# A longer token gather in the model that orders an attention and mixture-of-experts kernel

## The chip, the cores and the metric

The kernel runs on one core of one Trainium2 chip. A core has five engines that run side by side, each through its own list of instructions in a fixed order: TensorE (PE in the profile; its weight loads are PEld), VectorE (DVE), ScalarE (ACT), GpSimd (POOL) and SyncE (SP). They wait for each other by semaphores. Transfers are started by SP (hardware queue, q1) and by POOL (software queue, q0). The metric is device time in microseconds, median of several runs.

## The reference

Eight batches of eight heads of attention over 576 positions, half the heads with a window of 32, half with a dilated window of 128 with every fourth position; the result is a table of 4608 tokens of 512 numbers. A router then gives each token to one of eight experts of at most 576 tokens each, greedily by the largest logit, and each expert is a two-layer network:

```python
logits = x @ w_gate
order = np.argsort(-logits.flatten())
for idx in order:
    tok, e = (int(idx) // E, int(idx) % E)
    if assigned[tok] >= 0 or counts[e] >= cap:
        continue
    assigned[tok] = e
    counts[e] += 1
...
for e in range(E):
    mask = assigned == e
    out[mask] = np.maximum(x[mask] @ w1[e], 0.0) @ w2[e]
```

## The kernel before, in words

The first 230 us are attention. It leaves the tokens in a table `xd` in HBM and the logits on the chip. Then come eight rounds, one per expert.

In a round r the router **searches** which expert fills up next and down to which logit it accepts. The search is a chain that goes to and fro: TensorE counts (`pz<-G,ohr`, L782, nine small matmuls), VectorE narrows the interval (from `Q`, L819, to a new `G`, L796) and TensorE counts again, eight times. At its end VectorE makes the flags `ge` (L991) and the rank of each chosen token is counted on TensorE (L1028, L1029). VectorE turns ranks into places: `scan` (L1036) to `oa` (L1074), and six writes `ob` (L1087). GpSimd and ScalarE each scale half of `oa` into `rx` (L1079, L1083). Eighteen small matmuls `ptx<-rx,ob` (L1094) then put the token numbers in order; this is the **listing**. VectorE makes the index list `idx` of it (L1106).

GpSimd **gathers** the 576 tokens of the list from `xd` by five indirect transfers (`xg<-xd,idx`, L1258: four of 128 rows and one of 64). TensorE **turns** each of the five by four transposes into the one bank `ptx` (L1272); ScalarE copies it out as `xh` and VectorE writes the remainder `xl` (both by L1141 and L1142). A turn waits until the turn before it was copied out.

The **first product** is L1309: for each of eight slices f of the hidden layer, tokens 0 to 255 into `ph0` and 256 to 575 into `ph1`, twelve matmuls each (weights split in `w1h` and `w1l`, tokens in `xh` and `xl`). ScalarE and VectorE make `hb` of it (L1141, L1329). The **second product** is L1351: for each of five token blocks m and each f three matmuls into `py0` or `py1` in turn (L1354 and L1356 for the last block of 64). ScalarE copies `py` to `y` and GpSimd scatters it to the output (L1377).

The weights come from HBM into `raw` (SP, L1159). ScalarE makes the high half `w1h` or `w2h`; the low half is written by VectorE, or, in three cases among them both layers of the second expert, by a ScalarE copy (L1167) and an adding transfer of GpSimd (`w1l<-raw`, L1169). In the second round the loads of slices 4 to 7 of `w1` wait for a small memset on GpSimd (L1150, the gate) behind the second gather.

No order of instructions is written by hand. Every step is an `op` with an engine, an assumed cost, an assumed latency `lat` (after the engine is free again, until others see the result), the ops it depends on, and a boost. `Schedule.run` first goes through the ops backwards and gives each the time `left` to the end along its longest path; `due` is the end less `left` less the boost. Then it plays the engines forward in its own time: on each engine it takes the ready op with the earliest `due`, or another that fits in front of it. Whatever comes out of that is the order in which the instructions stand on the engines. `T_G` is the latency of the gathers in this model; it is in no instruction. The model takes 1250 ns of GpSimd for a gather, and then `lat`.

Of the kernel before, what the change touches and what calls it, by code (L numbers as in the profile page):

```python
# [37 lines left out]
T_P, T_S, AHEAD = 440, 2150, 5  # L38
B_L, B_G, B_T, B_X, B_H, B_HL, B_Y, B_S, B_W = 23000, 27000, 15000, 0, 20000, 17000, 28000, -15000, 1500
RAW1, D_R, NQ, AHEAD_W = 8, 262, (2, 2), (3, 4)  # L40
ADDED, T_A, T_G = (("2", 0), ("1", 1), ("2", 1)), 4500, 4500
NS, B_E, DIRECT = (2, 2), 3000, 7
B_C = (0, 2500, 20000, 20000, 20000, 20000, 20000, 20000)
P_U, B_A, B_K, B_V, B_P, TOL_A, TOL_B, TOL_C, TOL_D = 4680, 15400, -5200, 14500, -105500, 650, 650, 300, 800
# [111 lines left out]
class Schedule:  # L156
# [8 lines left out]
    def op(self, eng, cost, fn, deps=(), boost=0, lat=0, dma=0, buf=None):  # L165
        x = Op(len(self.ops), eng, cost, fn, deps, boost, lat, dma, buf)
        for d in x.deps:
            d.users.append(x)
        self.ops.append(x)
        return x  # L170
# [940 lines left out]
def moe(tc, ctx, C, R, xd, w1, w2, out):  # L1111
# [8 lines left out]
    op = K.op  # L1120
# [130 lines left out]
    def gather(r, ix, box):  # L1251

        done = []
        for m, n in enumerate(MSZ):
            xg, old, use = XG.take()

            def get(xg=xg, n=n, m=m):
                nc.gpsimd.indirect_dma_start(out=xg[:n], out_offset=None, in_=xd,  # L1258
                                             in_offset=bass.IndirectOffsetOnAxis(ap=box[0][:n, m:m + 1], axis=0))

            g = op("POOL", 1250, get, [ix, *old], B_G, lat=T_G if r else 2500)
            got[r, m] = g
            if r == 0:
                pt, old, usep = (PYR if m % 3 < 2 else PTR).take()
            else:
                pt, old, usep = PTR.take()
            pt = pt.rearrange("p (d x) -> p d x", d=ND)
            a, b = (x[:, :, 128 * m:128 * m + n] for x in (XH, XL))

            def turn(pt=pt, xg=xg, n=n):  # L1270
                for d in range(ND):
                    nc.tensor.transpose(pt[:, d, :n], xg[:n, 128 * d:128 * d + 128], C["identf"][:n, :n])  # L1272

            t = op("PE", 460 if n == 128 else 250, turn, [g, *old], B_T)
            use.append(t)
            if r == 0:
                turns.append(t)
            full = 500 if n == 128 else 290
            wx = x_users.get((r - 1, 0 if m < 2 else 1), [])
            s0 = op("ACT", full, lambda pt=pt, a=a, n=n: act(a, pt[:, :, :n]), [t, *wx], B_T)  # L1280
            s1 = op("DVE", full + 100, lambda pt=pt, a=a, b=b, n=n: sub(nc.vector, b, pt[:, :, :n], a), [s0], B_T)
            usep += [s0, s1]
            done.append((s0, s1))
        return done
# [107 lines left out]
    def round_(r):  # L1392
        e = None
        if r:
            e = search(r) if r < NE - 1 else chain("DVE", 650, R.last, [st["fetch"], st["need"]])
        en = st["fetch"] = EN[r] = op("SP", 100, lambda: fetch(r, R.eidx), [e])
        ix, BOX[r] = settle(r, e)
        X[r] = gather(r, ix, BOX[r])
        W[r] = [weights("1", r, f, [en]) for f in range(NF)]
# [85 lines left out]
```

## Time and profile before

| what | value |
|---|---|
| runs before | 704.34 us median of 3 (703.73 to 706.86) |
| the profiled execution | 708.44 us, of which the span of its instructions is 706.6 us |
| TensorE matmuls, weight loads | 665.0 us (94 %), 585.0 us (83 %) |
| VectorE, ScalarE, GpSimd | 484.7 us (69 %), 291.4 us (41 %), 140.6 us (20 %) |
| mean granted TensorE clock | 0.972 of full speed |

The profile comes from one execution. Times in it count from the start of its span. A row of the timeline has the start, the duration, the engine, the line, the operation and what it writes from what; in brackets stands how long the engine sat idle before it and what ended that. Matmuls overlap: their durations are longer than the distance from one start to the next, and it is the distance that adds up. The first round's tokens are turned from 236 us on, the first expert's products lie between 240 and 304 us, the second's between 304 and 357 us.

### The profile page before, as it was taken

To read this page: it belongs to the slowest core of one execution; us is meant where nothing else is said; L and a number is where in the kernel's file an instruction comes from. 1 tells how busy PE (TensorE), PEld (TensorE's weight loads), DVE (VectorE), ACT (ScalarE), POOL (GpSimd) and SP (SyncE) were. 2 spreads that over 40 slices of the span, in tenths; PEclk is the share of its full clock that TensorE was granted. 3 is DMA by queue.
4 is the path that set the end of the run, shared out by engine and by line. 5 is a ranking of instruction groups with operands and counts; after the bars stand their busy time and mean duration, and the time that the engine had idled before them with its cause. 6 is when DMAs were issued, how large, how long until landed. Compare 5 with 4: busy or idle time off the path is not lost.

```text
span 706.6 us, 17388 instructions
## 1 busy us (share of the span) xinstructions
PE 665.0 (94%) x6579; PEld 585.0 (83%) x6581; DVE 484.7 (69%) x2086; ACT 291.4 (41%) x616; POOL 140.6 (20%) x206
## 2 busy tenths in 40 slices
PE   7899999999974899899999999999999999999995
PEld 5787899888963698699889889879978988988983
DVE  5467877789457889588689879969978854724200
ACT  3344554453521474286335434423524525424210
POOL 6111111100000332452410410310321131211011
PEclk9999999999985899999999999999999999999998
DMA  9999999973211684889314514512711574113001
GB/s 253 266 265 284 279 311 255 264 202 80 63 41 45 194 177 112 249 174 268 98 53 137 180 51 130 185 43 73 239 51 53 164 261 147 50 58 98 1 23 45
DMA packets 58524, 104.60 MB, mean 148 GB/s; under 512 B 6212, under 2 KB 27844, under 8 KB 58436
## 3 DMA queue, kind: packets, MB, share of 16 engines
q1 hardware_dynamic: 49096, 78.32, 38.7%
q0 software_dynamic: 9344, 25.17, 13.4%
q8 instruction: 51, 0.84, 0.5%
q14 instruction: 33, 0.27, 0.1%
HBM read 78.31 MB, written 18.87 MB: 138 GB/s over the span
## 4 chain that ended last, share of the span: by engine, by line
PE 68%; issue 12%; DVE 10%; POOL 3%; DMA 3%; ACT 1%; another core or an unknown queue 1%; POOLq 0%; SPq 0%; DVEq 0%
PE py L1351 18%; PE ph L1309 17%; PE pS L506 9%; PE px L514 6%; PE px L564 3%; PE pS L503 3%; PE pm L486 2%; PE ptx L1272 2%; PE pz L782 2%; PE py L1354 1%; PE py L1356 1%; POOL out L1377 1%; DVE hb L1329 1%; DVE G L796 1%; DMA qs<-in_qd 1%
## 5 line engine op out<-in xcount | busy, mean ns | idle before, releaser
L1351 PE MATMUL py<-w2h,hb 128*128 128x512 f32 x512 | 172.0, 401 | 0.0
L1309 PE MATMUL ph<-xh,w1h 128*128 128x256 f32 (+1 forms) x512 | 138.1, 300 | 0.0
L1309 PE MATMUL ph<-xl,w1h 128*128 128x256 f32 (+1 forms) x512 | 136.8, 298 | 0.0
L1309 PE MATMUL ph<-xh,w1l 128*128 128x256 f32 (+1 forms) x512 | 136.0, 296 | 0.0
L1351 PEld LDWEIGHTS py<-w2h,hb 128*128 128x128 f32 x512 | 96.7, 189 | 19.4
L1351 PE MATMUL py<-w2l,hb 128*128 128x512 f32 x256 | 100.2, 392 | 0.0
L1141 ACT ACTIVATE hb<-ph 128x256 fp32r<-128x256 f32 (+2 forms) x192 | 59.6, 345 | 88.5 <-PE ph L1309 86.9
L1309 PEld LDWEIGHTS ph<-xh,w1h 128*128 128x128 f32 x512 | 91.8, 190 | 0.5
L1309 PEld LDWEIGHTS ph<-xh,w1l 128*128 128x128 f32 x512 | 91.8, 190 | 0.1
L1309 PEld LDWEIGHTS ph<-xl,w1h 128*128 128x128 f32 x512 | 91.4, 190 | 0.1
L506 PE MATMUL pS<-q,k 128*80 128x96 f32 (+1 forms) x672 | 83.0, 265 | 0.0
L1377 POOL DMA_INDIRECT out<-y,idx x40 | 41.3, 1034 | 194.6 <-ACT y L1141 136.0
L456 ACT ACTIVATE E<-pS 96x384 f32<-96x384 f32 (+1 forms) x96 | 46.5, 486 | 75.2 <-PE pS L506 74.1
L1329 DVE SCALAR_TENSOR_TENSOR hb<-ph,hb 128x320 fp32r<-128x320 f32 (+1 forms) x128 | 57.0, 452 | 29.4 <-ACT hb L1141 25.2
L506 PEld LDWEIGHTS pS<-q,k 128*80 128x80 f32 (+1 forms) x672 | 68.5, 158 | 0.0
L1141 ACT ACTIVATE y<-py 128x512 f32<-128x512 f32 (+1 forms) x40 | 23.8, 596 | 104.0 <-PE py L1351 90.5
L493 DVE CUSTOM_DVE_ANT_0 junkm<-pm,const 128x80 bf16<-128x80 f32 (+1 forms) x336 | 59.5, 244 | 4.2 <-PE pm L486 3.6
L1351 PEld LDWEIGHTS py<-w2l,hb 128*128 128x128 f32 x256 | 48.6, 190 | 8.5
L514 PE MATMUL px<-v,E 81*64 81x65 f32 (+1 forms) x1344 | 47.9, 225 | 5.3 <-issue 2.9
L1258 POOL DMA_INDIRECT xg<-xd,idx x40 | 42.1, 1054 | 52.7 <-PE ph L1309 25.1
L514 PEld LDWEIGHTS px<-v,E 81*64 81x64 f32 (+1 forms) x1344 | 42.8, 138 | 10.2 <-issue 3.8
L1141 ACT ACTIVATE w1h<-raw 128x512 fp32r<-128x512 f32 x64 | 39.6, 628 | 27.6 <-DMA raw<-in_moe_w 27.2
(179 smaller groups left out, 1009.5 us busy)
## 6 DMA issues: line engine op xcount, KB each, us to landing
raw<-in_moe_w SPq DMA_DIRECT2D x128, 256.0 KB, 4.6
v<-in_vp SPq DMA_DIRECT2D x8, 780.0 KB, 14.2
v<-in_vd SPq DMA_DIRECT2D x8, 650.0 KB, 10.3
xd<-xs SPq DMA_DIRECT2D x16, 288.0 KB, 7.5
xd<-xs SPq DMA_DIRECT2D x32, 144.0 KB, 9.2
w2l<-raw POOLq DMA_DIRECT2D x16, 256.0 KB
qs<-in_qp SPq DMA_DIRECT2D x7, 576.0 KB, 10.1
k<-in_kp SPq DMA_DIRECT2D x7, 576.0 KB, 9.7
```

What stands on the lines that cost most here:

```text
L456: e = self.op("ACT", 380, lambda j=j, pS=pS: nc.scalar.activation(self.E[:self.nk, j * self.gs:j * self.gs + self.gs], pS.tile[:, :self.gs ...
L493: nc.vector.tensor_tensor_reduce(out=jk[:, c - c0, :nk], in0=pm[:, (c - c0) * nk:(c - c0 + 1) * nk], in1=mm[:, min(1, (c if self.kind == 0 ...
L503: nc.tensor.matmul(pS[:nk, c - c0], ls[:64 + n, c], self.r[:64 + n, :2 * nq], start=(c == c0), stop=False, skip_group_check=True)
L506: nc.tensor.matmul(pS[:nk, c - c0], self.Ks[c], self.Qm[c], start=False, stop=True, skip_group_check=True)
L514: nc.tensor.matmul(px[64 * a:64 * a + 64, c - c0], lh, self.V[c][a], start=True, stop=True)
L564: nc.tensor.transpose(t[:, c], src, C["identf"])
L1141: act = lambda o, i, f=AF.Copy: nc.scalar.activation(o, i, f)
L1258: nc.gpsimd.indirect_dma_start(out=xg[:n], out_offset=None, in_=xd, in_offset=bass.IndirectOffsetOnAxis(ap=box[0][:n, m:m + 1], axis=0))
L1309: nc.tensor.matmul(o, a[:, d * 128:d * 128 + 128], b[:, d, c0:c1], start=((d, i) == pairs[0]), stop=((d, i) == pairs[-1]))
L1329: hl = op("DVE", 335 if j == 0 else 400, lambda: nc.vector.scalar_tensor_tensor(hb[:, CAP + c0:CAP + c1], o, 0.0, hb[:, c0:c1], op0=OP.max ...
L1351: nc.tensor.matmul(py, x, w, start=(f + i == 0), stop=(f == NF - 1 and i == 2))
L1377: s = nc.gpsimd.indirect_dma_start(out=out, out_offset=bass.IndirectOffsetOnAxis(ap=box[0][:n, m:m + 1], axis=0), in_=y[:n], in_offset=None)
```

## The change

The tuple `T_G` now holds three latencies: 2500 ns for the first round, as before, 7000 ns for the second, where it was 4500 ns, and 4500 ns for all later rounds, as before.

```diff
-ADDED, T_A, T_G = (("2", 0), ("1", 1), ("2", 1)), 4500, 4500
+ADDED, T_A, T_G = (("2", 0), ("1", 1), ("2", 1)), 4500, (2500, 7000, 4500)
...
-            g = op("POOL", 1250, get, [ix, *old], B_G, lat=T_G if r else 2500)
+            g = op("POOL", 1250, get, [ix, *old], B_G, lat=T_G[min(r, 2)])
```

The instructions are the same, 5688 rows on TensorE before and after. The order differs on TensorE, VectorE, ScalarE and GpSimd, on TensorE from the first expert's first product (some 249 us in the profile) to the second expert's second product (some 345 us); after that, and on SP throughout, it is the same. In the first product the last six of the eight counts L782 of the second round's search stand 12 to 18 matmuls earlier; the last of them stood behind the first three matmuls of the second product, and stands now behind the third matmul of the last group of the first product (`ph1`, f = 7).

On TensorE, the first expert's second product, before. `w2h6` and `hb6` are the weights and the hidden layer of slice f = 6, `py0` and `py1` the banks of the token blocks, `ge` the flags, `rx` and `ob` the listing's inputs; each pair of a weight and a hidden slice stands for three matmuls.

```order
L1351 MATMUL py0_3208<-w2h6_3237,hb6_3268 128x512
...
L1351 MATMUL py0_3208<-w2h7_3238,hb7_3269 128x512
...
L1028 MATMUL pz_81<-ge_4244,const4_64 128x72
...
L1351 MATMUL py1_3209<-w2h0_3231,hb0_3262 128x512
...
L1351 MATMUL py0_3208<-w2h0_3231,hb0_3262 128x512
...
L1094 MATMUL ptx0_3210<-rx_4289,ob_4293 128x40
```

And now:

```order
L1351 MATMUL py0_3208<-w2h4_3235,hb4_3266 128x512
...
L1028 MATMUL pz_81<-ge_4237,const4_64 128x72
...
L1351 MATMUL py0_3208<-w2h5_3236,hb5_3267 128x512
...
L1351 MATMUL py0_3208<-w2h6_3237,hb6_3268 128x512
...
L1094 MATMUL ptx0_3210<-rx_4273,ob_4277 128x40
...
L1351 MATMUL py0_3208<-w2h7_3238,hb7_3269 128x512
...
L1351 MATMUL py1_3209<-w2h0_3231,hb0_3262 128x512
```

The ranks L1028 moved up by three slices (nine matmuls), the listing L1094 by 30 matmuls. Between the two there were 27 matmuls, and there are six. The slice f = 7 of the first token block stands behind the listing. On VectorE the last write of `hb` for that slice (L1329, 128x320) stands now behind the six `ob`; it stood ahead of the search's last step.

On GpSimd, from the last adding transfer of the first expert to the gate of the second round (`raw_3215` is the buffer of slice 4); + and - are the difference from before to now, `y_3271` to `y_3273` are finished token blocks on their way out:

```order
 L1169 DMA w1l_3239<-raw_3211 128x512
 L1169 DMA w1l_3240<-raw_3212 128x512
 L1169 DMA w1l_3241<-raw_3213 128x512
-L1376 MEMSET spacer 1x1
-L1377 DMA out<-y_3272,idx 4608x512
 L1258 DMA xg_3255<-xd,idx 128x512
 L1258 DMA xg_3256<-xd,idx 128x512
...
+L1169 DMA w1l_3242<-raw_3214 128x512
+L1377 DMA out<-y_3271,idx 4608x512
+L1377 DMA out<-y_3272,idx 4608x512
 L1150 MEMSET raw_3215 1x1
```

The scatters of the first two token blocks stood ahead of the gathers, the first of them ahead of the three adding transfers as well; now both, and a fourth adding transfer, stand between the gathers and the gate.

On ScalarE, the copies `xh` of the turns among the second expert's weights, before (`raw14` to `raw16` are the slices f = 4 to 6, whose loads wait for the gate):

```order
L1141 ACTIVATE xh_3260<-ptx0_3210 128x4x128 x2
L1141 ACTIVATE w1h4_3227<-raw14_3215 128x512
L1141 ACTIVATE y0_3271<-py1_3209 128x512
L1167 ACTIVATE w1l4_3243<-w1h4_3227 128x512
L1141 ACTIVATE w1h5_3228<-raw15_3216 128x512
L1141 ACTIVATE xh_3260<-ptx0_3210 128x4x128
```

And now:

```order
L1141 ACTIVATE xh_3260<-ptx0_3210 128x4x128 x2
L1141 ACTIVATE y2_3273<-py0_3208 128x512
L1141 ACTIVATE w1h4_3227<-raw14_3215 128x512
L1141 ACTIVATE xh_3260<-ptx0_3210 128x4x128
L1167 ACTIVATE w1l4_3243<-w1h4_3227 128x512
L1141 ACTIVATE w1h5_3228<-raw15_3216 128x512
L1167 ACTIVATE w1l5_3244<-w1h5_3228 128x512
L1141 ACTIVATE w1h6_3229<-raw16_3217 128x512
L1141 ACTIVATE xh_3260<-ptx0_3210 128x4x128
```

The third copy `xh` stood behind the conversions of slices 4 and 5, and stands behind that of slice 4; the fourth stands behind that of slice 6, ahead of which it stood. The five turns themselves stand earlier in the second product on TensorE: the first is behind slice 3 of the third token block (it was behind slice 2 of the fourth), the fourth behind slice 3 of the fourth block.

## Rows read from the trace of the kernel before

**Rows 1.** The page: the span, and busy time by engine.

```profile
span 706.6 us, 17388 instructions
PE 665.0 (94%) x6579; PEld 585.0 (83%) x6581; DVE 484.7 (69%) x2086; ACT 291.4 (41%) x616; POOL 140.6 (20%) x206
```

**Rows 2.** The waits of TensorE: who waited for what, us in total, times, the longest. The first two are all that there is from 240 to 305 us, the third all from 305 to 345 us, the last all from 345 us to the end.

```profile
PE pz L782 <- DVE G L796: 2.7, 1, 2.7
PE ptx L1272 <- DVE xl L1142: 0.5, 1, 0.5
...
PE pz L1028 <- DVE ge L991: 0.6, 1, 0.6
...
PE ptx L1094 <- DVE ob L1087: 0.5, 2, 0.2
```

**Rows 3.** The chain that ended last, in order of time, around 290 us: start, us, what.

```profile
288.02 0.82 DVE G L796
...
288.98 3.63 another core or an unknown queue
```

**Rows 4.** Busy time by stretch: from and to, length, then busy us (and instructions) of PE, PEld, DVE, ACT and POOL, the granted TensorE clock, the DMA share, GB/s.

```profile
291.90:294.80 2.90, 0.24 (x2) 0.11 (x2) 1.98 (x9) 0.60 (x1) 0.35 (x1) 1.00 1.01 242
295.70:298.60 2.90, 2.89 (x9) 2.51 (x10) 2.45 (x10) 1.12 (x2) 0.00 (x0) 0.52 1.03 395
```

**Rows 5.** Timeline of TensorE.

```profile
262.46 0.45 PE L782 MATMUL pz<-G,ohr 128*128 128x64 bf16 x9
...
266.01 0.46 PE L782 MATMUL pz<-G,ohr 128*128 128x64 bf16 x9
...
268.86 0.39 PE L1351 MATMUL py<-w2h,hb 128*128 128x512 f32 x1
...
269.56 0.47 PE L782 MATMUL pz<-G,ohr 128*128 128x68 bf16 x9
...
274.05 0.39 PE L1351 MATMUL py<-w2h,hb 128*128 128x512 f32 x1
...
275.00 0.19 PE L1028 MATMUL pz<-ge,const 128*128 128x72 bf16 x1
...
275.06 0.47 PE L1351 MATMUL py<-w2h,hb 128*128 128x512 f32 x1
...
281.31 0.62 PE L1094 MATMUL ptx<-rx,ob 128*128 128x40 bf16 x18
281.78 0.48 PE L1351 MATMUL py<-w2h,hb 128*128 128x512 f32 x1
...
289.11 0.46 PE L782 MATMUL pz<-G,ohr 128*128 128x64 bf16 x9
289.41 0.63 PE L1272 MATMUL ptx<-const,xg 128*128 128x128 f32 x4
289.79 0.47 PE L1351 MATMUL py<-w2h,hb 128*128 128x512 f32 x1
...
291.72 0.40 PE L1351 MATMUL py<-w2h,hb 128*128 128x512 f32 x1
294.78 0.46 PE L782 MATMUL pz<-G,ohr 128*128 128x64 bf16 x9 [2.66 <-DVE G L796]
295.71 1.11 PE L1272 MATMUL ptx<-const,xg 128*128 128x128 f32 x4 [0.47 <-DVE xl L1142]
```

**Rows 6.** Timeline of VectorE.

```profile
269.64 0.49 DVE L1329 SCALAR_TENSOR_TENSOR hb<-ph,hb 128x320 fp32r<-128x320 f32 x1 [0.26 <-ACT hb L1141]
...
274.71 0.23 DVE L991 TENSOR_TENSOR ge<-te,gg 128x72 bf16<-128x72 f32 x1
...
277.45 3.50 DVE L1087 TENSOR_TENSOR ob<-si,const 128x384 bf16<-128x384 int32 x6
...
283.16 0.33 DVE L1106 SCALAR_TENSOR_TENSOR idx<-t 64x5 int32<-64x5 f32 x2
...
292.63 0.32 DVE L819 STREAM_TRANSPOSE Q<-pz 128x128 f32<-128x128 f32 x1 [3.65 <-remote]
...
294.97 0.68 DVE L1142 TENSOR_TENSOR xl<-ptx,xh 128x512 fp32r<-128x512 f32 x1
```

**Rows 7.** Timeline of ScalarE.

```profile
292.69 0.60 ACT L1141 ACTIVATE xh<-ptx 128x512 fp32r<-128x512 f32 x1 [4.83 <-remote]
...
297.35 0.63 ACT L1141 ACTIVATE w1h<-raw 128x512 fp32r<-128x512 f32 x1
```

**Rows 8.** Timeline of GpSimd.

```profile
283.84 1.03 POOL L1258 DMA_INDIRECT xg<-xd,idx  x1 [0.30 <-DVE A L1053]
...
289.86 0.09 POOL L1150 MEMSET raw<- 1x1 f32 x1
...
291.22 1.03 POOL L1377 DMA_INDIRECT out<-y,idx  x1 [0.27 <-issue]
```

**Rows 9.** SP's loads of weights: first the timeline (start, us until the next is issued), then the DMA view of 289 to 296 us (count, size of one, median us from issue to landing).

```profile
289.97 0.33 SPq L1159 DMA_DIRECT2D raw<-in_moe_w  x1
...
raw<-in_moe_w SPq DMA_DIRECT2D x8, 256.0 KB, 5.9
```

## The prediction

> **What bounds the kernel now.** I read the busy times first, then the waits of TensorE, then the timeline of the one stretch that the change reorders. TensorE is busy for 665.0 of 706.6 us [rows 1], and the list of its waits is short: 4.3 us in all from 240 us to the end, of which 0.5 us lie after 345 us [rows 2]. So the mixture-of-experts part is a queue of matmuls with next to no gaps, in which the search, the listing and the gathers of the next expert run beside the products of this one. From that two things follow. A better order has at most those few microseconds to win. And since the order after the second expert is the same as before and holds no slack (0.5 us of waits), what is lost in the changed stretch is not made up later.
>
> The largest wait is odd. At 288.98 us the chain names no engine for 3.63 us [rows 3]; VectorE (`Q`) sat idle for 3.65 us and ScalarE (`xh`) for 4.83 us, and both went on within 0.06 us of each other [rows 6, 7], though the count and the turn that they follow had begun at 289.11 and 289.41 us and last 0.46 and 0.63 us [rows 5]. TensorE ran out of work for it: 2.66 us without a matmul, until 294.78 us [rows 5]. From 295.70 to 298.60 us its granted clock was 0.52, against 1.00 around it: the lower of the two levels, 1.2 instead of 2.4 GHz. That cost 2.9 x 0.48 = 1.4 us more [rows 4]. Together 4.1 us.
>
> The profiled execution took 708.44 us: 706.6 us of span and 1.84 us around it. The median of the runs is 704.34 us, 4.1 us less. I therefore take it that the odd wait is an event of the profiled execution and not of the usual run, and count it out: 708.44 - 4.1 = 704.3 us is the base. That is a choice; the other reading is a rival below.
>
> **The change part by part.** The new latency costs nothing by itself, no instruction is added or gone. All that counts is where TensorE now meets a result that isn't there yet.
>
> *Units.* Between 275.06 and 281.31 us lie 27 matmuls of the second product, so one takes 0.2315 us; between the counts at 262.46 and 266.01 us lie 24 of the first product and one count of 0.30 us, so one takes 0.135 us; a turn takes 0.38 us, the listing 0.47 us (281.31 to 281.78) [rows 5].
>
> *The search, earlier.* The last count stood at 269.56 us, three matmuls into the second product. It now stands nine matmuls of 320 columns (by columns 0.15 us each, 1.3 us) and those three (0.7 us) earlier: 267.55 us, and the second product begins at 268.86 + 0.30 = 269.16 us. From the last count to the ranks L1028 the chain over VectorE took 275.00 - 269.56 = 5.44 us, so the ranks can be counted at 273.0 us. TensorE is at their new place after 15 matmuls, at 269.16 + 3.47 = 272.6 us, and waits 0.4 us. Whether VectorE can keep up with counts that come up to 2.4 us sooner is the unknown here: by its busy share it has little room, and if the search didn't get earlier at all, the ranks would come at 275.0 us as before and everything below 2.0 us later. I take the full 2.0 us, since VectorE waits for the count in this stretch more often than the count for VectorE.
>
> *The listing, too early.* From the ranks to the end of the six `ob` (277.45 + 3.50 = 280.95 us) VectorE needs 5.95 us [rows 5, 6], and the listing needs all six. Before, 27 matmuls (6.25 us) stood between, which covered it: the listing began at 281.31 us without a wait. Now six stand there, 1.39 us. TensorE has done them at 273.0 + 0.06 + 1.39 = 274.45 us, and the last `ob` is there at 273.0 + 5.95 = 278.95 us: a stop of 4.5 us, in which only the listing's own first matmuls run. Behind it stands slice 7 of the first token block, and it must wait for the last `hb`, which VectorE now writes after the `ob`, 0.49 us [rows 6]: it starts at 279.5 us. Before, it started at 274.05 us, with 0.80 us of work and wait still to come that now lies behind it (ranks 0.33 us with their wait, listing 0.47 us). TensorE is 279.5 - 274.05 - 0.8 = **4.65 us** late. Bounds: 4.0 us if VectorE is a little quicker, 6.7 us if the search gains nothing.
>
> *The clock.* The stop is longer than the one before 294.78 us, which was followed by 2.9 us at the lower level [rows 4, 5]. So the clock should fall here too. Part of the low stretch may lie in the stop itself, where it costs nothing, so the price is between 0 and 1.4 us; I take **1.0 us**, nearer to the row. The Trainium skill says the same against the change (TensorE: Matmul & The Clock Gate, section "Why this matters for your kernels": no gaps between bursts of matmuls, or the array falls back to the half clock); the trace agrees, with 0.52 after the one long gap. By that rule alone, with the low stretch wholly behind the stop, the sum would be 0.4 us higher.
>
> *The gathers and the gate.* The list `idx` came 1.7 us after the listing's end, with VectorE still at other work before it; the first gather was issued at 283.84 us, 2.06 us after that end [rows 5, 6, 8]. Now the listing ends at 279.05 us, so the first gather goes out near 280.9 us, three microseconds earlier. The turns need no gather for long: the first turn found its tokens 5.57 us after the issue (283.84 to 289.41) without a wait, and it will come at 290 us or later. So what 7000 ns stands for in the model costs TensorE nothing here, before or after.
>
> The gate is another matter. It stood right behind the gathers, 6.02 us after the first [rows 8]. Now an adding transfer and two scatters with their small memsets stand in front of it. From the gate to the end of the next scatter, 291.22 + 1.03 = 292.25 us, one adding transfer and one scatter took 2.39 us; with a second scatter of 1.3 us that is 3.7 us. The gate comes at 280.9 + 6.0 + 3.7 = 290.6 us, a little later than before (289.86 us), though the gathers are earlier. The load of slice 4 starts 0.1 us behind it and takes 5.9 us [rows 9]: 296.6 us. On ScalarE the third `xh` now stands behind the conversion of that slice, and the fourth turn needs it: 0.63 + 0.60 us on ScalarE [rows 7], 0.68 us for `xl` [rows 6], 0.2 us to hand over: 298.7 us. TensorE gets to the fourth turn after 63 matmuls (14.6 us), three counts and three turns (2.0 us) and the 1.0 us of clock: 279.5 + 17.6 = 297.1 us. It waits 1.6 us, less the 0.5 us for `xl` which the old order paid [rows 2]: **1.1 us**. Bounds: a gain of 0.5 us if the load is quick, 4 us if the load takes the 7.4 us from its issue to the conversion in the trace (289.97 to 297.35 us, where ScalarE was held up by the odd wait).
>
> *The second expert's first product.* Three counts of the third round's search stand closer together than before (the sixth to the seventh 20 matmuls apart instead of 28), and the ranks cost 0.6 us of wait before [rows 2]. I take **0.3 us**, bounds -0.6 and 1.5 us.
>
> Sum: 708.44 - 4.1 + 4.65 + 1.0 + 1.1 + 0.3 = 711.4 us, 7.0 us or 1.0 % over the median before.
>
> **The rivals.** A difference of 0.5 % is 3.5 us here, about what can be told from none: "same" is 700.8 to 707.9 us.
>
> *The odd wait belongs to every run before* (it stands between the search and the first turn, in a stretch of dense transfers), and the new order, which has other work there, doesn't meet it. Then the median of 704.34 us holds it, and the result is 704.34 - 4.1 + 7.05 = 707.3 us. For it: it hits two engines at one point of the order. Against: the 4.1 us between the profile and the median, and the lowest run, 703.73 us, is near it. Chance 0.17, half of it within "same", since its own error is some 1.5 us.
>
> *It is met again after, or the fourth turn waits for the long load*: 711.4 + 3 to 4 = 715 us. Chance 0.12.
>
> *The stop is a loan* (faster). The listing is late because its chain is; if the search were done by 268.5 us, the `ob` would be there at 274.45 us, TensorE would not stop, and the earlier gathers would clear the waits of 0.5 and 4.1 us: 704.3 - 0.5 = 703.8 us, or 699.7 us with the odd wait in the median. The mechanism is the whole search moving by 4.5 us more; it decides from a last count at 263.1 us. Against it: the place of that count in TensorE's list, which fixes it at 267.5 us or later. Chance 0.05.
>
> *The order changes and nothing shows*, because the work in the stretch is the same and other waits shrink by as much: 704.3 us. Waits of TensorE that could shrink are 4.3 us in all, most of it the odd one. Chance 0.06.
>
> **How the numbers follow.** The forecast, with its own range of 708.5 to 714 us, has 0.60. Of the last two rivals together (0.11) some 0.05 falls below 700.8 us: faster 0.05. Same: half of the first rival (0.085) and the other 0.065 of the last two: 0.15. Slower: the rest, 0.80. The range for 8 in 10 leaves out the last two rivals and the upper half of the second: 705.5 to 714.5 us.
>
> **What would show it.** In the profile after: TensorE idle for 4 to 5 us before L1094 near 274 to 279 us, named `ob` or `rx` as what ended it; a granted clock near one half for some of the 3 us after; a first gather near 281 us and a gate (L1150) near 290.6 us, behind two scatters; a wait of the fourth turn for `xl`, with ScalarE's conversion of slice 4 in front of `xh`; the second expert's first product beginning some 6 us later than in a run before without the odd wait, and no wait after 345 us that differs from before. I'm wrong if the listing starts without a stop, or if the later experts make the time good, or if the odd wait turns out to be in the usual run.

## The result, and the profile after

The changed kernel takes 711.0 us (median of 19 runs, 705.7 to 717.4) against 704.2 us of the kernel before on the same chip: the ratio is 1.0088, with a 95% interval of 1.0068 to 1.0109, so 4.8 to 7.7 us slower. The forecast was 711.4 us. Two more series of the same kernel on another chip gave 1.0102 (1.0063 to 1.0141) and 1.0088 (1.0057 to 1.0119).

The profiled execution of the changed kernel took only 705.72 us, with a span of 703.9 us; that of before took 708.44 us. The difference lies ahead of the change: the first round's ranks (L1028) stood at 220.51 us here and at 224.90 us in the profile of before, and over all profiles of this study they lie between 219.7 and 229.0 us whatever the kernel. So everything below is counted from these ranks. To set a time of this profile beside one of [rows 5 to 9], add 4.39 us to it.

The waits of TensorE in the kernel after, from 240 to 305 us (who waited for what, us in total, times, the longest):

```profile
PE ptx L1094 <- POOL rx L1079: 2.0, 1, 2.0
PE ptx L1094 <- DVE ob L1087: 1.1, 5, 0.2
PE pz L1028 <- DVE ge L991: 0.2, 1, 0.2
```

The wait of 2.7 us for `G` and that of 0.5 us for `xl` [rows 2] are gone; the listing waits in their place. TensorE's timeline there:

```profile
268.94 0.19 PE L1028 MATMUL pz<-ge,const 128*128 128x72 bf16 x1 [0.16 <-DVE ge L991]
...
270.23 0.39 PE L1351 MATMUL py<-w2h,hb 128*128 128x512 f32 x1
272.65 0.23 PE L1094 MATMUL ptx<-rx,ob 128*128 128x40 bf16 x3 [2.04 <-POOL rx L1079]
273.07 0.24 PE L1094 MATMUL ptx<-rx,ob 128*128 128x40 bf16 x3 [0.19 <-DVE ob L1087]
...
274.94 0.24 PE L1094 MATMUL ptx<-rx,ob 128*128 128x40 bf16 x3 [0.23 <-DVE ob L1087]
275.03 0.53 PE L1351 MATMUL py<-w2h,hb 128*128 128x512 f32 x1
```

The six matmuls behind the ranks are through at 270.46 us (270.23 us and the 0.23 us that one takes); the listing's 18 matmuls come in six small pieces, each as its `ob` is written, and the product goes on at 275.03 us. The stop lasts 4.57 us. The first and longest wait in it, 2.04 us, ends with `rx` of GpSimd, which starts as soon as VectorE has written `oa`; the five after it end with one `ob` each. The last `ob` is there at 274.89 us and so sets the end of the stop; `hb` and the list follow. VectorE and GpSimd (timelines):

```profile
271.39 3.50 DVE L1087 TENSOR_TENSOR ob<-si,const 128x384 bf16<-128x384 int32 x6
274.81 0.48 DVE L1329 SCALAR_TENSOR_TENSOR hb<-ph,hb 128x320 fp32r<-128x320 f32 x1
...
275.74 0.33 DVE L1106 SCALAR_TENSOR_TENSOR idx<-t 64x5 int32<-64x5 f32 x2
```

```profile
271.56 1.03 POOL L1079 TENSOR_TENSOR rx<-oa,const 128x360 bf16<-128x360 bf16 x1 [12.21 <-DVE oa L1074]
```

Behind the stop the clock is down. Busy time by stretch, columns as in [rows 4]; the granted clock is the third figure from the right:

```profile
270.46:275.00 4.54, 1.41 (x18) 0.84 (x18) 4.47 (x11) 4.38 (x8) 2.76 (x4) 1.00 0.65 170
275.00:277.50 2.50, 2.50 (x10) 1.96 (x11) 2.25 (x9) 1.42 (x3) 1.90 (x2) 0.56 1.00 166
277.50:280.00 2.50, 2.50 (x10) 2.00 (x9) 1.84 (x7) 1.16 (x1) 1.97 (x2) 0.75 0.87 200
280.00:283.00 3.00, 3.00 (x15) 2.48 (x14) 0.00 (x0) 0.00 (x1) 2.39 (x4) 1.00 0.66 193
```

That costs 2.5 x 0.44 + 2.5 x 0.25 = 1.7 us. Then the gathers, the gate and the loads; timeline of GpSimd, of SP, and the DMA view of 284 to 294 us, to be read beside [rows 8, 9]:

```profile
276.34 1.08 POOL L1258 DMA_INDIRECT xg<-xd,idx  x1 [0.52 <-DVE cap L1019]
...
285.43 0.97 POOL L1377 DMA_INDIRECT out<-y,idx  x1 [0.22 <-issue]
286.40 0.09 POOL L1150 MEMSET raw<- 1x1 f32 x1
```

```profile
raw<-in_moe_w SPq DMA_DIRECT2D x8, 256.0 KB, 4.6
```

The gate stands 10.06 us behind the first gather, after two scatters; the loads behind it took 4.6 us in the median, not 5.9, the first of them (slice 4, which the fourth turn needs) 3.2 us, and no turn waits. From the first ranks to the end of the span this execution took 483.4 us, that of before 481.7 us, although the latter holds the odd wait of [rows 3].

### The profile page after: what moved, and what is told of

It reads as the page before. It is cut to its first block, busy times and chain, and to the rows that moved or that the text cites. A ratio compares the mean times of both kernels' runs of the same rounds, so it can differ in the third digit from the quotient of the medians.

```text
span 703.9 us, 17394 instructions
## 1 busy us (share of the span) xinstructions
PE 665.7 (95%) x6581; PEld 583.5 (83%) x6581; DVE 484.4 (69%) x2086; ACT 292.0 (41%) x616; POOL 140.8 (20%) x206
## 4 chain that ended last, share of the span: by engine, by line
PE 65%; DVE 12%; issue 11%; DMA 6%; POOL 2%; ACT 1%; SPq 0%; POOLq 0%; DVEq 0%
PE py L1351 19%; PE ph L1309 15%; PE pS L506 8%; PE px L514 5%; DMA qs<-in_qd 3%; PE px L564 3%; PE pS L503 2%; PE pm L486 2%; PE ptx L1272 2%; DVE hb L1329 2%; PE py L1354 2%; PE py L1356 2%; PE pz L782 1%; DVE G L796 1%; DMA v<-in_vd 1%
## 5 line engine op out<-in xcount | busy, mean ns | idle before, releaser
L1329 DVE SCALAR_TENSOR_TENSOR hb<-ph,hb 128x320 fp32r<-128x320 f32 (+1 forms) x128 | 56.7, 452 | 27.4 <-ACT hb L1141 26.1
```

Of the source, the lines that this page charges most:

```text
L1329: hl = op("DVE", 335 if j == 0 else 400, lambda: nc.vector.scalar_tensor_tensor(hb[:, CAP + c0:CAP + c1], o, 0.0, hb[:, c0:c1], op0=OP.max ...
```

## A ledger of TensorE's losses

For each profile of this study the time from 14 us behind the first ranks to the start of the third expert's first product was divided into windows of 1 us, and two things were summed: the time in which TensorE ran no matmul ("idle"), and busy time x (1 - granted clock) ("clock"). 44 to 62 us is the stretch of the second round's ranks and listing, 62 to 85 us that of the turns and their loads, 85 to 112 us the third round's ranks and listing. All in us; the labels are those of the experiments below. The last column counts from the first ranks.

| kernel (label) | 44-62 idle | clock | 62-85 idle | clock | 85-112 idle | clock | third expert starts |
|---|---|---|---|---|---|---|---|
| before, first profile | 0.1 | 0 | 3.3 | 1.5 | 0.6 | 0 | 138.25 |
| before (e4) | 0.1 | 0 | 0.5 | 0 | 1.9 | 0 | 136.02 |
| before (e12) | 0.1 | 0 | 1.8 | 1.7 | 0.4 | 0 | 136.99 |
| after, first profile | 3.3 | 1.7 | 0 | 0 | 1.5 | 0 | 140.74 |
| after (e5) | 3.2 | 3.1 | 0 | 0 | 1.5 | 1.7 | 143.15 |
| after (e9) | 3.3 | 3.1 | 0 | 0 | 1.1 | 0 | 141.82 |
| gate early (e6) | 3.3 | 1.6 | 0 | 0 | 1.5 | 0 | 140.96 |
| zeros (e3) | 0.3 | 0 | 4.2 | 0 | 0.9 | 0 | 142.51 |
| zeros (e10) | 0.3 | 0 | 4.3 | 0 | 0.8 | 0 | 142.59 |
| zeros, gate early (e7) | 0.3 | 0 | 0 | 0 | 1.5 | 1.6 | 140.69 |
| zeros, gate early (e11) | 0.4 | 0 | 0 | 0 | 1.2 | 0 | 139.00 |
| hb first (e1) | 0 | 0 | 0.2 | 0 | 3.5 | 0 | 137.24 |
| 5500 ns (e2) | 0.1 | 0 | 0.3 | 0 | 1.4 | 0 | 136.60 |
| 9000 ns (e8) | 1.4 | 1.7 | 0 | 0 | 1.0 | 0 | 139.38 |

Take off idle and clock, and the 0.2 to 1.1 us of idle time between 14 and 44 us that the table leaves out: 132.4 to 134.1 us are left in the rows without zeros and 136.5 to 136.9 us in those with them. So the ledger closes to 1.7 us. (The listing counts 1.4 us where it comes in six pieces and 0.6 us where it comes in one, which is about half of that spread.)

## The experiments

**The stop taken away, the 7000 ns kept (e1).** The model ranks the last `hb` of the token block ahead of the listing's chain, and so puts the listing some 33 matmuls behind the ranks:

```diff
-                hb[:, CAP + c0:CAP + c1], o, 0.0, hb[:, c0:c1], op0=OP.max, op1=OP.subtract), [hh], B_HL)
+                hb[:, CAP + c0:CAP + c1], o, 0.0, hb[:, c0:c1], op0=OP.max, op1=OP.subtract), [hh], B_HL + (40000 if (r, f) == (0, NF - 1) else 0))
```

> The kernel after, with one number of the order changed: the last part of the hidden values (hb, L1329) of the last slice of the first token block is ranked ahead of the listing's chain, so that the model lets the listing's matmuls (L1094) stand some 33 matmuls behind the ranks (L1028) instead of 6. The latency of 7000 ns stays, and with it the place of the first turns and of the gate. Theory (the stop of TensorE ahead of the listing, 4.6 us, and the clock of 0.56 and 0.75 behind it, 1.7 us, make the whole difference): no wait of TensorE above 0.5 us between 265 and 285 us, granted clock 0.97 to 1.00 there, and the time of the kernel before within 1.5 us, 702.7 to 705.7 us. Rival 1 (the gathers, scatters, gate and turns in their new order cost by themselves): the stop goes and the time stays 2 us or more above that of before, 706.2 to 709 us. Rival 2 (what is saved is asked back later, by waits of the second expert): 709 to 711 us.

Measured: 706.7 us beside 706.0 us for before in the same series, ratio 1.0009 (0.9977 to 1.0041). TensorE's timeline shows ranks and listing without a wait, the listing in one piece:

```profile
273.28 0.19 PE L1028 MATMUL pz<-ge,const 128*128 128x72 bf16 x1
...
280.94 0.62 PE L1094 MATMUL ptx<-rx,ob 128*128 128x40 bf16 x18
```

The time of before is back, as far as the interval tells, with the clock at 1.00 from the first expert's products to the third expert. So the loss comes with the stop, as the theory has it; rival 2 falls, and of rival 1 no more than the interval's upper end of 2.9 us is left. A part of what is saved is asked back: the third round's ranks and listing cost 3.5 us of idle time here. This order still has two scatters between the gathers and the gate, and the gate comes even later than in after (67.6 us behind the first ranks, not 65.9), so a late gate alone costs little. The gathers are not those of after, though: they go out 58.4 us behind the first ranks, 2.6 us later.

**Another latency, 5500 ns (e2).**

```diff
-ADDED, T_A, T_G = (("2", 0), ("1", 1), ("2", 1)), 4500, (2500, 7000, 4500)
+ADDED, T_A, T_G = (("2", 0), ("1", 1), ("2", 1)), 4500, (2500, 5500, 4500)
```

> The kernel after with 5500 ns for the second round's gather instead of 7000. The order then puts the ranks (L1028) behind slice 6 of the second product and the listing (L1094) 27 matmuls or more behind them. Theory (the stop ahead of the listing and the clock behind it make the difference): no stop, clock 0.97 to 1.00 between 270 and 285 us, time of the kernel before within 2 us, 702 to 706 us. Rival (every order in which that search is brought forward pays for it, in waits for VectorE or for the later gate): 706.5 to 710 us.

Measured: 706.6 us in the same series, ratio 1.0010 (0.9975 to 1.0044); no stop, clock 1.00. This order brings the ranks forward by three matmuls only, where after has nine, and in time they come no earlier than in before (50.6 us behind the first ranks, not 50.1). So it shows that the rest of the new order is free without the stop, and not what an earlier search alone would do.

**9000 ns: a shorter stop (e8).** The same line with 9000.

> The kernel after with 9000 ns instead of 7000: the order brings the search forward further and puts 15 matmuls (3.5 us) between the ranks and the listing instead of 6 (1.4 us). Theory (TensorE's loss is the time from the ranks to the last ob, 5.95 us, less the work in between): a stop of 2.2 to 2.8 us, a clock that falls less or not at all, and 2 to 4 us under after. Rival (the loss comes with the order of the whole stretch, not with the stop): the time of after within 1 us, or above it.

Measured: 709.1 us, ratio 1.0060 (1.0034 to 1.0087). TensorE arrives as the first `ob` are there and has no wait over 0.23 us, but the listing is drawn out over 2.39 us (277.86 to 280.25 us):

```profile
277.86 0.23 PE L1094 MATMUL ptx<-rx,ob 128*128 128x40 bf16 x3
...
280.16 0.24 PE L1094 MATMUL ptx<-rx,ob 128*128 128x40 bf16 x3 [0.23 <-DVE ob L1087]
280.25 0.48 PE L1351 MATMUL py<-w2h,hb 128*128 128x512 f32 x1
```

Windows of the same stretch:

```profile
277.86:280.25 2.39, 1.29 (x20) 0.78 (x19) 2.39 (x6) 2.33 (x5) 1.64 (x2) 1.00 0.54 99
280.25:282.75 2.50, 2.50 (x11) 1.76 (x11) 2.29 (x9) 1.51 (x3) 1.73 (x2) 0.74 0.98 163
282.75:285.25 2.50, 2.50 (x8) 1.97 (x7) 2.10 (x8) 0.87 (x1) 1.89 (x3) 0.58 0.79 184
```

The stop is half as long, as it should be with 9 more matmuls (2.1 us) in between. By the medians the kernel lies between before and after, 4.1 us under after, though the upper end of its interval overlaps that of after in the same series (1.0063 to 1.0141). The clock fell in this profile too and cost 1.7 us, as much as in the first profile of after. Over the twelve runs the mean granted clock is 0.9728, against 0.9690 of after and 0.9729 of before in the same series, so on average it costs less than behind the longer stop, as expected.

**The stop filled with zeros (e3, e10).** 18 matmuls of zeros, whose products nobody reads, stand right ahead of the second round's listing:

```diff
+        if x is listed.get(1):
+            keep_clock(nc, R.zero, fill, 18)
```

> The kernel after, and 18 matmuls of zeros into a bank that is free, right ahead of the listing's matmuls (L1094) of the second round: some 4 us of work for TensorE in the stop, whose products nobody reads. Theory (1.7 of the 6.3 us are the clock, which falls because TensorE stands still): the stop in the profile shrinks to under 1.5 us, the granted clock stays 0.95 or more in the 5 us behind it, and the time is 1 to 2 us under that of after in the same runs, about 709.3 us. Rival 1 (the clock falls for another reason, the power of the stretch, and the zeros don't help): clock below 0.8 again and the time of after within 0.5 us. Rival 2 (the zeros run longer than the stop and delay the listing): 0.5 to 2 us over that of after.

> The run with the 18 matmuls of zeros ahead of the listing, again, on one chip with the kernel after. Theory (the zeros keep the clock, and what the clock gives is partly lost to the late loads): a mean granted clock like that of before within 0.001, and a time 0.5 to 2 us under after. Rival 1 (the clock is worth nothing, since the loads end last in any case): the time of after within 0.5 us. Rival 2 (the clock is worth all of its 1.7 us and more): over 2 us under after.

Measured: 710.7 us, ratio 1.0075 (1.0044 to 1.0106), and 711.8 us, ratio 1.0087 (1.0059 to 1.0115), beside 1.0088 (1.0057 to 1.0119) for after on the same chip. In the profile of e3 the zeros fill the stop, and the clock stays up; TensorE's timeline and one window:

```profile
275.44 3.83 PE L121 MATMUL ph<-zero 128*128 128x512 bf16 x17
279.10 0.83 PE L1094 MATMUL ptx<-rx,ob 128*128 128x40 bf16 x18
279.78 0.48 PE L1352 MATMUL py<-w2h,hb 128*128 128x512 f32 x1
```

```profile
279.30:281.80 2.50, 2.45 (x26) 1.99 (x23) 2.29 (x9) 2.03 (x4) 1.89 (x3) 1.00 0.99 165
```

The Trainium skill asks for this (TensorE: Matmul & The Clock Gate, section "Why this matters for your kernels": no idle gaps between bursts of matmuls); these rows agree, 1.00 with the gap filled and 0.56 without. The timed runs agree as well: their mean granted clock is 0.9728 in e10, against 0.9702 of after and 0.9738 of before in the same series. Yet the time gained at the first turn (63.74 us behind the first ranks, in after 65.48 us) is gone at the fifth. TensorE's row, and ScalarE's:

```profile
302.44 0.46 PE L1273 MATMUL ptx<-const,xg 64*128 64x64 f32 x4 [2.37 <-DVE xl L1142]
```

```profile
300.55 0.63 ACT L1141 ACTIVATE w1h<-raw 128x512 fp32r<-128x512 f32 x1 [3.05 <-DMA raw<-in_moe_w]
301.08 0.58 ACT L1141 ACTIVATE xh<-ptx 128x512 fp32r<-128x512 f32 x1
```

The turn waits for `xl`, this for `xh`, and `xh` stands on ScalarE behind a conversion whose load is late: it took 6.6 us here and 6.3 us in e10, where the same load of after took 4.5 us. So the turn waits both because TensorE is earlier and because this load is slower; what makes it slower is not shown. The next round's search, started late, then makes its first count wait 1.84 us for `G` (2.16 us in e10). Both runs lose 4.2 to 4.3 us there. The gain of 1 to 2 us (e3) or 0.5 to 2 us (e10) does not show in the medians, though intervals of some 2 us on either side do not exclude it. In the profiles the clock is kept, and the time isn't.

**The gate ahead of the scatters (e6), and with the zeros (e7, e11).** Only the second gather gets 4500 ns again; TensorE's order stays word for word, GpSimd's gate goes ahead of the two scatters (and its second and third gather change places):

```diff
-            g = op("POOL", 1250, get, [ix, *old], B_G, lat=T_G[min(r, 2)])
+            g = op("POOL", 1250, get, [ix, *old], B_G, lat=T_G[min(r, 2)] if (r, m) != (1, 1) else 4500)
```

> The kernel after, with the second of the five gathers given 4500 ns again in the model: TensorE's order stays word for word that of after, but GpSimd issues the gate (L1150) ahead of the two scatters instead of behind them, so that the loads of slices 4 to 7 start some 2.4 us earlier. Theory (the price is the stop and the clock, and the late loads cost nothing or only now and then): the time of after within 1.5 us. Rival (in the usual execution the late gate makes a turn wait, as with the zeros): 1.5 to 3 us under after, and no wait of a turn for xl in the profile.

> The run with the zeros and the early gate together. In the run with the zeros TensorE came to the fifth turn 1.8 us earlier than in after (74.5 instead of 76.3 us from the first round's ranks), as the clock would have it, and then waited 2.37 us for xl, whose xh stood on ScalarE behind a conversion that waited 3.05 us for its load. Theory (the clock's 1.7 us are real, and the late loads eat them): with the loads earlier the turn waits less than 0.7 us and the time is 1.2 to 2.5 us under after. Rival (the 1.7 us are lost again elsewhere in the second expert whatever the loads do): the time of the run with the zeros, less than 1 us under after.

> Zeros and early gate, again, on one chip with the two others. Theory (the early gate takes away the wait of the turn): 0 to 1.5 us under the run with the zeros alone. Rival (the gate costs or gives nothing that can be told): within 0.5 us of it, on either side.

Measured: the gate alone 712.9 us, ratio 1.0116 (1.0076 to 1.0155), so no gain that can be told, as its theory had it; no turn waited in after, and none waits here. With the zeros 709.6 us, 1.0092 (1.0058 to 1.0126), and 709.2 us, 1.0073 (1.0047 to 1.0099). In the profile of e11 GpSimd's gate and first scatter, and the fifth turn:

```profile
286.40 0.44 POOL L1150 MEMSET raw<- 1x1 f32 x1
...
287.11 1.05 POOL L1378 DMA_INDIRECT out<-y,idx  x1 [0.24 <-issue]
```

```profile
298.28 0.46 PE L1273 MATMUL ptx<-const,xg 64*128 64x64 f32 x4
```

The turn waits in neither run. In the mean of two profiles each the third expert starts 139.8 us behind the first ranks, against 142.6 us with the zeros alone and 141.9 us in the three profiles of after. So in the ledger clock plus gate are worth 2 us, and the gate nothing without the clock (141.0 us in e6, no earlier than the first profile of after). In the timed runs the medians are 3.6 us (e7) and 2.2 us (e11) under after, and 2.7 us under the zeros alone, more than the 1.5 us expected; but the intervals overlap, so there it stays undecided.

**The same kernels again (e5, e9, e4, e12).**

> The kernel after, unchanged, beside the next three on one chip: for its time there, and for a second profile of the stretch. Theory (stop of 4.6 us and a clock of 0.56 and 0.75 in the 5 us behind it, in every execution): both again within 0.3 us; 4.8 to 7.7 us over the kernel before, as the interval of the first comparison has it. Rival (the low clock belonged to the one profiled execution): clock above 0.9 behind the stop. Whether the fourth or fifth turn (L1272) waits for xl, as it did by 2.37 us in the run with the zeros and not at all in the first profile of after, is looked at too.

> The kernel after, unchanged, on the same chip as the next two: the base for the question what of its loss is the clock. Theory (1.7 us of the loss are the clock behind the stop, the rest the stop): 5.5 to 8 us over the kernel before, and a mean granted clock over all runs that is 0.002 to 0.004 under that of before.

Measured: 713.2 and 711.4 us, ratios as told at the top. The stop is there each time (3.2 to 3.3 us idle). The clock is dearer than in the first profile: it falls already in the stop and stays at 0.50 for 5 us behind it, where the first profile had 0.56 and 0.75. So "within 0.3 us" held for the stop and not for the clock. In e5 it fell a second time, behind the third round's listing. Windows of e5:

```profile
273.40:274.87 1.47, 0.89 (x12) 0.55 (x13) 1.47 (x4) 1.44 (x4) 0.87 (x1) 0.51 0.83 143
274.87:277.37 2.50, 2.50 (x9) 2.02 (x9) 2.23 (x9) 1.47 (x3) 1.94 (x2) 0.50 0.99 165
277.37:279.87 2.50, 2.50 (x7) 1.92 (x7) 1.80 (x6) 1.16 (x1) 2.02 (x2) 0.50 0.81 190
279.87:282.37 2.50, 2.50 (x12) 2.01 (x11) 0.00 (x0) 0.00 (x0) 1.89 (x3) 0.93 0.66 203
328.00:331.00 3.00, 3.00 (x15) 3.00 (x16) 2.75 (x10) 0.90 (x3) 0.56 (x1) 0.50 0.08 31
```

Over all runs the mean granted clock is 0.9690 (e5) and 0.9702 (e9), against 0.9729 and 0.9738 of before. That is 0.0036 to 0.0039 of some 710 us, 2.6 to 2.8 us; the three profiles each of the ledger differ by 2.1 us.

> The kernel before once more, unchanged, for a second profile. Theory (the wait of 3.63 us that names no engine belongs to the one profiled execution): no idle time over 1.5 us on VectorE and ScalarE together around the first turn (L1272), no fall of the clock behind it, and from the first round's ranks (L1028) to the end of the span 477.6 us, 4.1 us less than in the first profile. Rival (it belongs to every execution of before): the wait is there again at the same place, 2 to 4 us, and that stretch lasts 481 to 482 us. The load of slice 4 of the first weights, 5.9 us in the first profile, is looked at too: near 4.6 us, as in the profile of after, if the odd wait or its transfers had lengthened it.

> The kernel before, unchanged, a third profile. Theory (the 3.63 us that name no engine were an event of the first profiled execution): no such wait, 478 to 480 us from the first round's ranks to the end of the span, the third expert's first product 135.5 to 136.7 us behind those ranks (138.25 in the first profile, 136.02 in the second). Rival (it comes back in a good part of the executions): the wait again, 137.5 us or more.

Measured: in e4 nothing odd; 479.0 us from the first ranks to the end, against 477.6 expected and 481.7 in the first profile. The gain is less than 4.1 us because waits come back that the odd wait had covered: the third round's ranks wait 0.89 us and its listing 1.1 us (before: 0.6 and 0 [rows 2]). The loads took 6.4 us, not 4.6. In e12 (699.5 us of span, 479.8 us behind the ranks) the odd wait is there again, smaller. TensorE, VectorE and ScalarE:

```profile
284.13 0.63 PE L1272 MATMUL ptx<-const,xg 128*128 128x128 f32 x4
...
288.05 0.45 PE L782 MATMUL pz<-G,ohr 128*128 128x64 bf16 x9 [1.20 <-DVE G L796]
```

```profile
285.89 0.32 DVE L819 STREAM_TRANSPOSE Q<-pz 128x128 f32<-128x128 f32 x1 [2.41 <-PE ptx L1272]
```

```profile
285.95 0.60 ACT L1141 ACTIVATE xh<-ptx 128x512 fp32r<-128x512 f32 x1 [3.37 <-PE ptx L1272]
```

As in [rows 6, 7] `Q` and `xh` go on 0.06 us apart and late: the turn that they follow began at 284.13 us and lasts 0.63 us. A clock of 0.51 follows, as in [rows 4]. The third expert starts 136.99 us behind the first ranks, between the two forecasts. The theory that the odd wait belonged to one execution falls; that it belongs to every one falls by e4.

## Why the prediction was right, and where it was not

*The stop.* 4.65 us were forecast. By the same count, slice 7 goes on 275.03 - 220.51 = 54.52 us behind the first ranks, in before 274.05 - 224.90 = 49.15 us [rows 5]; less the 0.80 us that lay behind it, 4.57 us. Right, and e1 and e2 show that without it the time is that of before. Its details held too: ranks 48.4 us behind the first ones (forecast 48.1), first gather 55.8 (56.0), gate 65.9 (65.7). One step in it was wrong and did no harm: slice 7 of the first token block, tokens 0 to 127, does not wait for the last `hb`, which writes tokens 256 to 575. It went on at 275.03 us while that write ran until 275.29 us. The 0.55 us forecast for this wait were made up, in part, by ranks that came 0.3 us later.

*The clock.* Mis-sized: 1.0 us forecast, bounds 0 to 1.4. Behind the stop it took 1.7, 2.7 and 2.7 us in the three profiles of after and 1.5 us in e6 (windows from the product's first matmul on). What failed is the length of the low stretch, taken from a window of 2.9 us [rows 4]. That window begins too late: in the profile of before the clock is down from 295.08 us on, 3.4 us in all.

```profile
295.08:295.70 0.62, 0.16 (x5) 0.02 (x1) 0.62 (x2) 0.00 (x0) 0.00 (x0) 0.50 1.07 373
```

The first profile of after has 3.4 us too, all of it behind the stop. In e5 and e9 the low stretch lasts 6.8 us: 1.5 us of it lie in the stop, as the prediction thought possible, and 5.4 us behind it.

*The fourth turn.* 1.1 us forecast, 0 measured in the three profiles of after and in e6. The gate was as late as forecast, but the load of slice 4 took 3.2 to 3.8 us in the profiles of after, not 5.9, and landed 69.2 us behind the first ranks in the first of them, not 71.7. The mechanism is real and lies close behind: with TensorE 1.7 us earlier and a slower load it cost 2.1 to 2.4 us at the fifth turn (e3, e10), and an earlier gate took it away.

*The base.* The odd wait was counted out of the profile as an event of that one execution. Two of three profiles of before have it (62 to 85 us: 4.8, 0.5 and 3.5 us lost), none of eight with after's order on TensorE, zeros or not. So the choice of the base was wrong in part, and the first rival holds in part: the median of before contains some of the odd wait, and the new order, where it was not met, wins that back. In the mean of three profiles each that stretch lost 2.9 us before and nothing after. The half of the second rival by which the odd wait is met again after falls.

*The second expert.* 0.3 us forecast; the third round's stretch cost 1.3 us of idle time after and 1.0 us before, in the mean of three each, and e5 and e7 lost 1.6 to 1.7 us to the clock there as well.

So the stop was forecast rightly, but that the total was met within 0.4 us is luck: the odd wait that the new order wins back and the turn that didn't wait are offset by a dearer clock and the third round. In the mean of three profiles each the third expert starts 141.90 us behind the first ranks after and 137.09 us before: 4.8 us later. Idle time at the stop is +3.15, clock there +2.6, the stretch of the turns -2.9, the third round +0.35 and +0.55; 0.4 us lie ahead of 44 us, and the 0.7 us that are left fit the listing in six pieces. From there to the end all six profiles take 342.6 to 343.6 us, so nothing is made good later, as forecast, and the rivals of the loan and of the order that shows nothing fall. The runs say 6.2 to 7.2 us; the 1.4 us and more between are within what three profiles, which differ by 2.2 to 2.4 us among themselves, can tell, and stay unassigned.

## What to carry to other kernels

Where one engine has no slack, a planner's latency matters by what it lets the planner put ahead of that engine's next wait: here a longer gather set the listing six matmuls behind the ranks instead of 27, where neither `rx` nor its six `ob` were written yet. Price such a stop with the clock behind it, and then look for the transfer that is hidden only because the stop is there: in the profiles, filling the stop kept the clock and gained nothing until the loads were moved too. And a wait that one profile can't name is to be looked for in further profiles of the same kernel before it is counted in or out.

## What was not expected of the hardware

The clock's low stretch at the same stop had two lengths, 3.4 us (first profile of after, e6) and 6.8 us (e5, e9), and in one profile it also followed a listing that was merely drawn out (2.39 us in e8). Behind the third round's listing it came in two of fourteen profiles (e5, e7). That listing lasted 2.7 and 2.8 us there from its first piece to its last, and 2.9 us in e6 and 3.0 us in e1, where the clock stayed up.

The late hand-over of count and turn to VectorE and ScalarE is not explained. It was met only where the first turn begins 5.5 to 5.6 us behind the issue of its gather (283.84 to 289.41 us [rows 5, 8], and 278.67 to 284.13 us in e12), not at 5.7 us (e4) nor at 6.3 to 11.6 us in the others. A turn that in truth waits for its tokens while the records show it running would fit that, and would make the longer latency right in itself, but it is not shown. In the twelve other profiles the first gather landed 3.7 to 5.3 us after its issue; in these two the trace holds no landing of it. Against it stands that the count, which reads no tokens, was handed over as late as the turn, 0.06 us ahead of it (0.47 us in e4, where nothing was late). A kernel that moves this turn alone was not tried.

One kind of load, the 256 KB of a weight slice behind the gate, took between 4.3 us (e5, the same kernel as after with 4.6) and 7.0 us (e10) in the median; what sets it stays open.
